# Issuing five of eight W1 slices of a fused attention and feed-forward kernel from ScalarE's DMA queue instead of SyncE's

## The chip, the core and the metric

The kernel runs on one NeuronCore of a Trainium2 chip. The core has five engines that run lists of their own and meet through semaphores: TensorE (PE in the profile), VectorE (DVE), ScalarE (ACT), GpSimd (POOL) and SyncE (SP, which here only issues DMAs). Data moves between HBM and on-chip memory through 16 DMA engines; SyncE, ScalarE and GpSimd each have a queue to them. The metric is device time in microseconds (us) of one execution; lower is better.

## What is computed

A linear-attention recurrence over 768 steps, for 4 batches and 8 heads of width 48, and then a feed-forward layer with a squared ReLU on its output:

```python
for t in range(S):
    kt, vt, rt = (k[:, :, t], v[:, :, t], r[:, :, t])
    cur = einsum('bhd,bhe->bhde', u[None] * kt, vt)
    y[:, :, t] = einsum('bhd,bhde->bhe', rt, state + cur)
    state = w[None, :, :, None] * state + einsum('bhd,bhe->bhde', kt, vt)
x = y.transpose(0, 2, 1, 3).reshape(3072, 384)
h = maximum(x @ w_in, 0.0)          # w_in: 384 x 2048
out = h * h @ w_out                 # w_out: 2048 x 384
```

Inputs and the output are float32 in HBM.

## The kernel before

The 768 steps are cut into 6 chunks of 128, and each pair of a chunk and a batch is a unit: 24 units, unit i being chunk i // 4 of batch i % 4. A unit loads its r, k and v (`ld`, line 319; 192 KB each, in runs of 192 bytes), scales r and k by powers of the decay (`rh`, `kh`, lines 335 to 339), transposes them on TensorE (`T`) with a copy back by ScalarE (`Tc`), multiplies (`A`), masks the product on VectorE (`Bm`), multiplies with v in bfloat16 (`vb`, then `Y`), and adds the diagonal term, which comes from `P0`, `P1`, `du` and `dv` (`xs`). The 128 x 384 result is transposed (`X`, `xTc`) and enters the feed-forward layer: `F1` (line 438) multiplies with W1, `re` and `sq` make the squared ReLU, `F2` (line 466) multiplies with W2, `os` and `out` bring it out. `U`, `S0`, `ts` and `S` keep the state for the next chunk. Units 0 and 1 are feed-forward groups of their own, later units go in pairs.

W1 lies on chip as eight bfloat16 slices of 256 columns. Slice 2 comes by a GpSimd DMA that converts (`W.0.2`). Slices 0, 1, 3, 4, 5, 6 and 7 come in float32, 384 KB each (`lW.0.s`, line 322), into one of four staging buffers (`wsa`, the number after the slash), and are converted by an engine (`cW.0.s`, line 326; ScalarE, but GpSimd for slice 7). A staging buffer is loaded again only after its copy: slice 7 follows 6 in buffer 0, 4 follows 1 in buffer 1, 3 follows 0 in buffer 2. `F1.g.s` of group 0 or 1 needs slices 2s and 2s + 1 of W1: `F1.1.0` needs 0 and 1, `F1.1.3` needs 6 and 7, and its second half only 7. W2 comes by GpSimd DMAs (`W.1.q`).

The order of all the work is written out by hand in `ORDER` (lines 20 to 106). Each word is a step, its indices, a colon and its engine (A ScalarE, D VectorE, G GpSimd, P TensorE, S SyncE), and after a slash the buffers that it takes: `lW.0.6:S/0` issues the load of slice 6 on SyncE into buffer 0. The loop at line 498 goes through the words and appends each step to its engine's list:

```python
for step in ORDER.split():
    what, how = step.split(":")
    ...
    getattr(Do, name)(E[eng[0]], *at, *map(int, eng[1:]))
```

So an engine works its steps strictly in the order of the words that name it, waiting at each for what it needs, and what stands behind a waiting step waits too. `Z.n.b` (line 479) are n filler matmuls that keep TensorE running in the opening. Units 1, 0, 2 and 3 are worked first, in that order. On SyncE the loads of the opening stand in this order: r.1, k.1, u, k.0, k.2, r.0, r.2, slice 6, v.1, k.3, v.3, slice 1, r.3, v.0, v.2, slices 0, 5, 7, 4, `wc`, k.4, slice 3, r.4. On ScalarE: `w` (a DMA of 6 KB), `tab` (a table load), `logw`, `Wt`, `Wk`, `Tc.1`, `WtS`, `WkS`, `Tc.0`, `cW.0.6`, `Tc.2`, `vb.1`, `cW.0.1`, `vb.3`, `xTc.1`, `vb.0`, `Tc.3`, `cW.0.0`. On GpSimd, after its constants: `P1.1`, `P0.2`, `dv.1`, `P1.0`, `P0.3`, `vb.2`, `P1.3`, `dv.2`, `W.1.0`, `W.0.2`, `cW.0.7`. On TensorE the attention of units 1, 0, 2, 3 with its fillers, ending in `Y.0`, `Z.13`, `A.3`, `X.0`, `U.0`, `Z.6`, and then `F1.1.0`, `F1.0.0`, `Y.2`, `Y.3`, `F1.1.3`.

In the built program the DMAs of SyncE and ScalarE share eight completion semaphores. They take them in turn, and a DMA that gets a semaphore first waits until the DMA that held it before has landed.

Of the kernel before, what the change touches and what calls it, by code (L numbers as in the profile page):

```python
# [17 lines left out]
EARLY = 4  # L18
POOLS = dict(ldr=7, ldk=7, ldv=7, ws=0, wsa=4, rk=7, P0=5, dv=5, vb=8, rkT=7, bank=4, bankH=2, bankO=2, Bm=6, xs=5, xT1=2, xT2=3, xT4=1, hr=6, hq=30, os=4, ts=2)
ORDER = """  # L20
ld.r.1:S/0 w:A ld.k.1:S/0 u:S Z.48.5:P tab:A ld.k.0:S/1 ld.k.2:S/2 shw:D ld.r.0:S/1 logw:A ld.r.2:S/2 Wt:A/0 P0.1:D/0
shu:D Wk:A/1 lW.0.6:S/0 rh.1:D/0 kh.1:D ld.v.1:S/0 ld.k.3:S/3 T.1:P/0 kh.0:D/1 Z.16.5:P P1.1:G Tc.1:A/0 kh.2:D/2 rh.0:D
ld.v.3:S/1 WtS:A rh.2:D P0.2:G/1 A.1:P/1/2 WkS:A T.0:P/3 lW.0.1:S/1 Z.16.5:P P1.2:D ld.r.3:S/3 Tc.0:A/1 du.1:D/0
P0.0:D/2 cW.0.6:A ld.v.0:S/2 A.0:P/0/3 dv.1:G Bm.1.1:D/0 Z.6.5:P du.2:D/1 T.2:P/2 P1.0:G Bm.1.0:D/1 ld.v.2:S/3 Z.22.5:P
Tc.2:A/2 Bm.0.0:D/2 Bm.0.1:D/3 lW.0.0:S/2 vb.1:A/0 lW.0.5:S/3 kh.3:D/3 Y.1:P/1 cW.0.1:A lW.0.7:S/0 A.2:P/0/2 xs.1:D/0
Z.4.5:P P0.3:G/3 vb.3:A/1 du.0:D/2 lW.0.4:S/1 X.1:P/3 Z.8.5:P rh.3:D wc:S xTc.1:A/0 Bm.2.0:D/4 vb.0:A/2 T.3:P/1
ld.k.4:S/4 dv.0:D Y.0:P/3 Z.13.5:P Tc.3:A/3 vb.2:G/3 Bm.2.1:D/5 P1.3:G xs.0:D/1 A.3:P/0/2 X.0:P/1 cW.0.0:A U.0:P/3
dv.2:G Bm.3.0:D/1 Z.6.7:P xTc.0:A/1 du.3:D/3 lW.0.3:S/2 F1.1.0:P/0 Bm.3.1:D/0 ld.r.4:S/4 F1.0.0:P/1 re.1.0:D/0 W.1.0:G
# [80 lines left out]
    A=["bA{0}0", "bA{0}1"],  # L109
    ld=["{0}{1}"],  # L110
    lW=["ws{0}{1}"], kh=["rk{0}"], rh=["rk{0}"], P0=["P{0}"], du=["dv{0}"], vb=["vb{0}"], T=["bT{0}"], Tc=["rkT{0}"], XB=["rkT{0}"],
    Bm=["Bm{0}{1}"], Y=["bY{0}"], xs=["xs{0}"], U=["bU{0}"], ts=["ts{0}"], X=["bX{0}"], re=["hr{0},{1}"], sq=["hq{0},{1}"],
# [429 lines left out]
```

## Time and profile before

| | us |
|---|---|
| median of 3 runs | 175.31 (175.0 to 175.56) |
| the profiled execution: from its first to its last instruction (span) | 174.6 |
| so around the span, against the median of the runs | 0.7 |
| TensorE busy | 164.3 (94% of the span) |
| VectorE busy | 140.6 (80%) |
| ScalarE busy | 109.4 (63%) |
| GpSimd busy | 69.4 (40%) |

The profiled execution's own time is known by its span alone. TensorE's granted clock is 0.998 of full speed over the span. The profile's page gives busy times, the span in 40 slices, the chain of work that ended last and the costliest groups of instructions, named by the line of the code; other views list instructions in order of time, each engine's waits with what ended them, and busy times and DMA traffic of any stretch. A DMA's issue is on its issuing engine's list with the letter q (SPq, ACTq); the transfer itself lands some us later. In the chain of work that ended last, TensorE has 84% of the span and the loads of the staging buffers 6%, all in the opening.

### The profile page before, as it was taken

Reading aid. Unit: us, or ns where it says so; the run is one execution under the profiler, and the core shown is the slowest. Engines: PE = TensorE matmul, PEld = TensorE weight load, DVE = VectorE, ACT = ScalarE, POOL = GpSimd, SP = SyncE. Lnnn points to the kernel's source line nnn. Section 1 sums busy time; section 2 is a strip of 40 time slices with the busy share of each in tenths; the row PEclk is TensorE's granted clock in tenths of the full one; section 3 lists DMA queues with packets and bytes.
Section 4 is the critical chain, followed back from the end, with each engine's and each line's share of the span. In section 5 each row is a group of like instructions: output and inputs, shape, how many; then the busy total and the mean of one; then the engine's idle time right before and its main releaser. Section 6 shows DMA issues by size and latency. Waiting matters only on the chain.

```text
span 174.6 us, 4605 instructions
## 1 busy us (share of the span) xinstructions
PE 164.3 (94%) x1813; PEld 127.1 (73%) x1813; DVE 140.6 (80%) x279; ACT 109.4 (63%) x203; POOL 69.4 (40%) x85
## 2 busy tenths in 40 slices
PE   3978599999999999999999999999999999999991
PEld 3967488866778777877767787777778677787760
DVE  5779677799899989999989898899988667853620
ACT  3578479549499987786677669669478142164410
POOL 5253834044366594925373960700950302000000
PEclk9999999999999999999999999999999999999999
DMA  4989999989799999999998989989931422110041
GB/s 99 228 194 240 320 200 237 207 155 213 144 205 177 231 217 165 233 157 252 152 214 187 195 164 220 160 196 230 164 94 26 158 90 71 24 45 4 0 165 61
DMA packets 102421, 28.36 MB, mean 162 GB/s; under 512 B 94840, under 2 KB 102400, under 8 KB 102400
## 3 DMA queue, kind: packets, MB, share of 16 engines
q1 hardware_dynamic: 100504, 26.20, 72.6%
q0 software_dynamic: 1744, 1.77, 6.3%
q8 instruction: 14, 0.23, 0.5%
q10 hardware_dynamic: 152, 0.10, 0.2%
q14 instruction: 7, 0.06, 0.1%
HBM read 20.46 MB, written 4.72 MB: 144 GB/s over the span
## 4 chain that ended last, share of the span: by engine, by line
PE 84%; DMA 6%; SPq 4%; POOL 1%; issue 1%; ACT 0%; DVE 0%; POOLq 0%
PE bank L472 36%; PE bank L445 36%; DMA wsa<-in_moe_w_in_dram 6%; SPq L320 4%; PE bank L376 3%; PE bank L394 2%; PE bank L392 2%; PE bank L403 2%; PE bank L363 2%; PE bank L429 1%; POOL W L262 1%; SPq L324 0%; POOL urow L218 0%; ACT vb L260 0%; DVE os L262 0%
## 5 line engine op out<-in xcount | busy, mean ns | idle before, releaser
L445 PE MATMUL bank<-xT,W 128*128 128x256 bf16 (+1 forms) x624 | 74.4, 264 | 2.3 <-ACT W L260 2.1
L472 PE MATMUL bank<-W,hq 128*128 128x384 bf16 x384 | 73.6, 326 | 0.0
L453 ACT ACTIVATE hr<-bank 128x512 bf16<-128x512 f32 x71 | 42.0, 597 | 36.8 <-PE bank L445 34.2
L445 PEld LDWEIGHTS <-W 128*128 128x128 bf16 x624 | 55.4, 98 | 12.6 <-ACT W L260 2.2
L472 PEld LDWEIGHTS <-hq 128*128 128x128 bf16 x384 | 35.6, 98 | 17.8
L460 ACT ACTIVATE hq<-hr 128x512 bf16<-128x512 bf16 x57 | 34.7, 629 | 2.5 <-DVE hr L455 2.2
L384 DVE TENSOR_TENSOR Bm<-bank,maskJT 128x512 bf16<-128x512 f32 x48 | 31.4, 682 | 3.1 <-PE bank L376 3.0
L346 POOL TENSOR_TENSOR P<-P,ub 128x384 f32<-128x384 f32 x14 | 15.2, 1087 | 30.2 <-DVE P L342 27.4
L354 POOL TENSOR_TENSOR dv<-ldv,du 128x384 f32<-128x384 f32 x19 | 16.4, 874 | 25.0 <-DVE du L349 21.0
L455 DVE TENSOR_SCALAR hr<-bank 128x512 bf16<-128x512 f32 x25 | 17.1, 688 | 11.2 <-PE bank L445 7.5
L464 DVE TENSOR_TENSOR hq<-hr 128x512 bf16<-128x512 bf16 x35 | 15.0, 456 | 1.7 <-ACT hr L453 1.7
L411 DVE TENSOR_TENSOR xs<-bank,dv 128x384 bf16<-128x384 f32 x24 | 13.2, 553 | 3.2 <-PE bank L394 2.5
L481 PE MATMUL bank<-identity 128*128 128x128 bf16 x139 | 11.1, 244 | 2.7 <-POOL identity masks.py:199 2.7
L260 ACT COPY os<-bank 128x384 f32<-128x384 f32 (+1 forms) x18 | 8.4, 469 | 8.1 <-PE bank L472 8.1
L342 POOL TENSOR_TENSOR P<-ldr,ldk 128x384 f32<-128x384 f32 x11 | 11.3, 1025 | 4.8 <-DMA ldr<-in_r_dram 4.8
L349 DVE TENSOR_REDUCE du<-P 128x8 f32<-128x384 f32 x24 | 12.9, 542 | 0.0
L260 ACT COPY rkT<-bank 128x1024 bf16<-128x1024 bf16 x10 | 10.1, 1016 | 3.4 <-PE bank L363 3.3
L481 PEld LDWEIGHTS <-identity 128*128 128x128 bf16 x139 | 9.8, 112 | 2.9 <-POOL identity masks.py:199 2.7
L424 POOL TENSOR_TENSOR S0W<-ts,WLm 128x384 bf16<-128x384 f32 x7 | 7.4, 1061 | 10.0 <-PE bank L472 6.7
L394 PE MATMUL bank<-vb,Bm 128*128 128x48 bf16 x192 | 10.8, 183 | 0.5 <-ACT vb L260 0.5
L394 PEld LDWEIGHTS <-Bm 128*128 128x128 bf16 x192 | 9.5, 96 | 1.5 <-issue 0.8
L260 ACT COPY xT<-bank 128x384 bf16<-128x384 bf16 x14 | 6.5, 478 | 5.1 <-PE bank L429 5.1
(62 smaller groups left out, 167.1 us busy)
## 6 DMA issues: line engine op xcount, KB each, us to landing
ldr<-in_r_dram SPq DMA_DIRECT2D x24, 192.0 KB, 3.8
ldk<-in_k_dram SPq DMA_DIRECT2D x24, 192.0 KB, 3.9
ldv<-in_v_dram SPq DMA_DIRECT2D x24, 192.0 KB, 3.6
out_dram<-os SPq DMA_DIRECT2D x23, 192.0 KB, 2.1
wsa<-in_moe_w_in_dram SPq DMA_DIRECT2D x7, 384.0 KB, 5.9
W<-in_moe_w_out_dram POOLq DMA_DIRECT2D x4, 384.0 KB, 7.6
rkT<-rk SPq DMA_TRANSPOSE x14, 4.2
W<-in_moe_w_in_dram POOLq DMA_DIRECT2D x1, 192.0 KB, 8.8
```

The lines of the kernel that those rows point to most:

```text
L260: e.copy(o, a)
L346: e.tensor_mul(t, t, ub)
L354: e.tensor_mul(dvb[slot[f"dv{i}"]], loaded("v", i), t)
L384: e.tensor_mul(Bmb[slot[f"Bm{i}{h}"]], heads(bank(f"bA{i}{h}"), 128), mask_b)
L394: e.matmul(y[:, hc, D * h : D * (h + 1)], m[h][:, hc, :], vb[:, 2 * hc + h, :], start=(c == 0), stop=True, skip_group_check=True,)
L445: e.matmul(hp[:, fi, :], W1[f // 2][:, c, 128 * (f % 2) : 128 * (f % 2 + 1)], xt[:, c, :], start=(c == 0), stop=(c == CCH - 1), skip_group ...
L453: e.activation(hr, hp, AF.Relu)
L455: e.tensor_scalar_max(hr, hp, 0.0)
L460: e.activation(hq, hr, AF.Square)
L464: e.tensor_mul(hq, hr, hr)
L472: e.matmul(bank(f"bO{i}", "bO")[:, 0:d_model], hqb[slot[f"hq{g},{f // m}"]][:, at : at + L], W2[q][:, f % 4, :], start=(f == 0), stop=(f = ...
L481: e.matmul(banks[b][:, 0:128], identity, identity, start=True, stop=True, skip_group_check=True)
```

## The change

Five words of `ORDER` move: the loads of slices 6, 1, 0, 7 and 5 are issued by ScalarE, at new places. All other words keep their order, the buffers are the same, and SyncE still issues slices 4 and 3.

```diff
-ld.r.1:S/0 w:A ld.k.1:S/0 u:S Z.48.5:P tab:A ld.k.0:S/1 ld.k.2:S/2 shw:D ld.r.0:S/1 logw:A ld.r.2:S/2 Wt:A/0 P0.1:D/0
-shu:D Wk:A/1 lW.0.6:S/0 rh.1:D/0 kh.1:D ld.v.1:S/0 ld.k.3:S/3 T.1:P/0 kh.0:D/1 Z.16.5:P P1.1:G Tc.1:A/0 kh.2:D/2 rh.0:D
-ld.v.3:S/1 WtS:A rh.2:D P0.2:G/1 A.1:P/1/2 WkS:A T.0:P/3 lW.0.1:S/1 Z.16.5:P P1.2:D ld.r.3:S/3 Tc.0:A/1 du.1:D/0
-P0.0:D/2 cW.0.6:A ld.v.0:S/2 A.0:P/0/3 dv.1:G Bm.1.1:D/0 Z.6.5:P du.2:D/1 T.2:P/2 P1.0:G Bm.1.0:D/1 ld.v.2:S/3 Z.22.5:P
-Tc.2:A/2 Bm.0.0:D/2 Bm.0.1:D/3 lW.0.0:S/2 vb.1:A/0 lW.0.5:S/3 kh.3:D/3 Y.1:P/1 cW.0.1:A lW.0.7:S/0 A.2:P/0/2 xs.1:D/0
+ld.r.1:S/0 w:A ld.k.1:S/0 u:S Z.48.5:P tab:A lW.0.6:A/0 ld.k.0:S/1 ld.k.2:S/2 shw:D ld.r.0:S/1 logw:A ld.r.2:S/2 Wt:A/0
+P0.1:D/0 shu:D Wk:A/1 lW.0.1:A/1 rh.1:D/0 kh.1:D ld.v.1:S/0 ld.k.3:S/3 T.1:P/0 kh.0:D/1 Z.16.5:P P1.1:G Tc.1:A/0
+kh.2:D/2 rh.0:D ld.v.3:S/1 WtS:A rh.2:D P0.2:G/1 A.1:P/1/2 WkS:A lW.0.0:A/2 T.0:P/3 Z.16.5:P P1.2:D ld.r.3:S/3 Tc.0:A/1
+du.1:D/0 P0.0:D/2 cW.0.6:A lW.0.7:A/0 ld.v.0:S/2 A.0:P/0/3 dv.1:G Bm.1.1:D/0 Z.6.5:P du.2:D/1 T.2:P/2 P1.0:G Bm.1.0:D/1
+ld.v.2:S/3 Z.22.5:P Tc.2:A/2 Bm.0.0:D/2 Bm.0.1:D/3 vb.1:A/0 lW.0.5:A/3 kh.3:D/3 Y.1:P/1 cW.0.1:A A.2:P/0/2 xs.1:D/0
```

On ScalarE the issues now stand behind `tab` (slice 6), `Wk` (1), `WkS` (0), `cW.0.6` (7) and `vb.1` (5). The lists of TensorE, VectorE and GpSimd are the same instruction by instruction. Since the semaphores go round in another order, the five issues wait, by the built program, for these landings: slice 6 for none, slice 1 for k.2, slice 0 for r.2, slice 7 for v.1 (and for the copy `cW.0.6`), slice 5 for k.3.

## The prediction

> **What bounds the kernel now.** I read the page's busy times first, then TensorE's waits in two halves, then the opening's timeline engine by engine, then windows of the opening for the DMA queues.
>
> TensorE is busy 164.3 of 174.6 us. Its waits, asked for 0 to 24 us and for 24 us to the end, say where the rest lies:
>
> ```profile
> PE bank L481 <- POOL identity masks.py:199: 2.7, 1, 2.7
> PE bank L445 <- ACT W L260: 2.1, 1, 2.1
> PE bank L363 <- DVE Bm L384: 0.6, 1, 0.6
> PE bank L394 <- ACT vb L260: 0.5, 2, 0.3
> PE bank L376 <- ACT rkT L260: 0.4, 2, 0.2
> ...
> PE bank L445 <- POOL W L262: 0.3, 1, 0.3
> ```
>
> The last row is the only wait after 24 us. From then on TensorE simply works through its list, so whatever moves that instant moves the end by as much. What ends last there are two copies of W1 slices, and behind each a load. In the timeline (start, duration, engine, what; in brackets the idle time before it and who ended it):
>
> ```profile
> 15.00 0.88 ACT L260 CAST W<-wsa 128x768 bf16<-128x768 f32 x1 [0.47 <-DMA wsa<-in_moe_w_in_dram]
> 20.70 0.86 ACT L260 CAST W<-wsa 128x768 bf16<-128x768 f32 x1 [2.61 <-DMA wsa<-in_moe_w_in_dram]
> 21.63 1.51 PE L445 MATMUL bank<-xT,W 128*128 128x128 bf16 x24 [2.06 <-ACT W L260]
> 23.23 0.87 POOL L262 CAST W<-wsa 128x768 bf16<-128x768 f32 x1 [1.93 <-DMA wsa<-in_moe_w_in_dram]
> 24.15 0.51 PE L445 MATMUL bank<-xT,W 128*128 128x128 bf16 x6 [0.27 <-POOL W L262]
> ```
>
> These are cW.0.1, cW.0.0, F1.1.0 with F1.0.0, cW.0.7 and the second half of F1.1.3. TensorE ended its fillers at 19.57 (19.07 + 0.50) and waited 2.06 us for slice 0.
>
> The other engines tell how much room there is. VectorE is gap-free from 10.33 to 20.43 (10.08 busy in 10.10), and what starts this stretch is unit 2's r:
>
> ```profile
> 9.18 0.55 DVE L339 TENSOR_TENSOR rk<-ldr,bank 128x384 bf16<-128x384 f32 x1 [0.61 <-DMA ldr<-in_r_dram]
> 9.30 1.00 POOL L342 TENSOR_TENSOR P<-ldr,ldk 128x384 f32<-128x384 f32 x1 [2.44 <-DMA ldr<-in_r_dram]
> 10.33 0.56 DVE L346 TENSOR_TENSOR P<-P,ub 128x384 f32<-128x384 f32 x1 [0.59 <-POOL P L342]
> 17.38 0.58 POOL L262 CAST vb<-ldv 128x384 bf16<-128x384 f32 x1 [0.45 <-DMA ldv<-in_v_dram]
> ```
>
> A late ld.r.2 shifts every VectorE instruction up to Bm.3.1. The last row is GpSimd's own chain: ld.v.2 lands, then vb.2, P1.3, dv.2, W.1.0, W.0.2 run back to back to 21.30, and cW.0.7 stands behind them.
>
> Windows of the opening (last numbers: granted clock, share of the 16 DMA engines, GB/s):
>
> ```profile
> 2.00:7.50 5.50, 4.79 (x53) 4.80 (x54) 4.91 (x20) 2.89 (x4) 2.01 (x7) 1.00 0.99 199
> 10.50:12.00 1.50, 1.13 (x20) 0.73 (x18) 1.50 (x4) 1.35 (x2) 0.24 (x1) 1.00 0.57 116
> 14.50:16.50 2.00, 1.85 (x35) 1.53 (x34) 2.00 (x6) 1.53 (x4) 0.57 (x1) 1.00 1.16 233
> 17.00:21.00 4.00, 2.26 (x42) 1.81 (x41) 3.41 (x7) 1.39 (x3) 3.62 (x5) 1.00 0.96 305
> ```
>
> The DMA engines are full nearly all the time, except for a hole at 10.5 to 12. In front of it stands SyncE's issue of ld.v.3, which took 2.71 us where most others took 0.4 to 0.8; the last row of this fence is ScalarE's only DMA of the opening:
>
> ```profile
> 8.10 2.71 SPq L320 DMA_DIRECT2D ldv<-in_v_dram  x1
> 1.25 1.08 ACTq L274 DMA_DIRECT2D wrow<-in_w_dram  x1
> ```
>
> **The change part by part.** No byte and no compute instruction is added; TensorE's, VectorE's and GpSimd's lists are the same. Five issues leave SyncE and join ScalarE, where four of them come much earlier among the loads.
>
> *What goes.* Slices 6, 1, 0, 7 and 5 no longer stand behind twelve r, k, v loads. If all five landed in time and nothing else moved, F1.1.0 would start at 19.57 and the second half of F1.1.3 2.24 us later (before: F1.1.0 at 21.63, F1.1.3 at 23.38, its second half 0.49 on, without its 0.27 wait), at 21.81. GpSimd could start cW.0.7 at 21.30 and end it at 22.17. So the second half starts at 22.2 instead of 24.15: at most 1.93 us gained, with GpSimd's chain late next.
>
> *What is pushed.* A slice costs 1.29 us of the DMA engines (393,216 bytes at the 305 GB/s of 17 to 21 us, when only slices flowed). How many go ahead of which load follows from the waits of the built program. There are eight completion semaphores for both queues, and a DMA waits for the landing of the one that last held its own. lW.0.6 waits for none. lW.0.1 waits for ld.k.2 (issued 3.16, 3.7 to landing, so 6.8 now), lW.0.0 for ld.r.2 (9.1), lW.0.7 for ld.v.1 and for cW.0.6, lW.0.5 for ld.k.3. So only slice 6 gets ahead of r.2: its landing moves by 0.4 to 1.3 us, the low end if the two queues together reach the share of 1.16 that 14.5 to 16.5 shows, instead of 0.99 over some 5 us. I take 1.3, since the trace has no two such queues together. Ahead of v.2 stand four slices instead of two: 2.58 us more, less the hole, which ScalarE's queue can fill (0.43 of 1.5 us, 0.65): 1.93 at the old share. At 1.16 all the way (0.15 of some 15 us is 2.2) nothing is left of it. Between 0 and 1.93 I take 1.15, a little nearer to the full price, for the rows that have r, k and v alone lie at 0.99 more often than at 1.16.
>
> *What ScalarE pays.* Five issues. SyncE's seven slice issues took 0.42 to 0.88, median 0.70. lW.0.6 lies in the idle time before logw (ScalarE's table load starts at 2.36, logw at 4.28). lW.0.1 waits for k.2, about 7.9, and puts off Tc.1 from 7.88 to about 8.6; what needs it, A.1 and then Bm.1.1, runs at 11.73 plus the 1.3 above. lW.0.0 waits for r.2 (10.4) and puts Tc.0 at 11.1, ending 12.1; cW.0.6 ends at 13.0, lW.0.7 at 13.7. T.2 needs the bank that Bm.1.1 frees (12.41 + 1.3), so Tc.2 could start at 14.4 (13.11 + 1.3) anyway: these are hidden. lW.0.5 is not: behind it stand cW.0.1, vb.3, xTc.1, vb.0 and Tc.3, and Y.0 (17.23, waiting for vb.0), A.3, X.0 and the fillers follow. The 0.47 us that ScalarE idled before cW.0.1 goes with the early slice, the issue takes 0.70: 0.23 net.
>
> *Sum.* TensorE's line: 21.81 + 1.30 + 0.23 = 23.35. GpSimd's: 22.17 + 1.15 + 0.05 to start = 23.4. The later sets it: 23.4 for 24.15, a gain of 0.75, and TensorE has no wait behind it. W.0.2, issued 1.1 us later on GpSimd, has lands at 29.3 now and is needed near 31, in a stretch with fewer slices left to move: I cost it nothing; without that cover some tenths. The trace's span is 174.64; the runs' median lies 0.67 above it, which I keep. 175.31 - 0.75 = 174.56, say **174.6**.
>
> **The rivals.**
>
> *Pushed at full price.* The queues share the same engines and gain nothing by being two: v.2 lands 1.93 late, cW.0.7 ends at 24.1, and the time is **175.3**. For it: a share of 0.96 to 0.99 in two of the four windows. Against it: the hole, and 1.16. The Trainium skill, DMA: Bandwidth & Descriptors, section "Issuing engines are not separate DMA queues", says just this: issuers interleave on the same 16 engines, and only issue time is saved. By that rule the sum is 175.3; by the 1.16 row it is 174.6 or less.
>
> *ScalarE stuck in its issues (slower).* A compute engine now waits wherever SyncE waited. ScalarE's one DMA moved 6 KB and still took 1.08 us, while SyncE issued ld.k.1 and u in the same time; the two issues of wc took 0.48 and 0.53 alone. If issues go one at a time, and SyncE sits in one for 2.71 us, lW.0.5 may take 2.7 instead of 0.7, and all of the 2.0 stands on TensorE's line: 23.35 + 2.0 = 25.35, that is 1.2 us slower, **176.5**. It decides from an issue of lW.0.5 above 1.5 us (the gain of 0.75 used up). For it: that row, and that pushed loads fill SyncE's queue sooner. Against it: SyncE is done with ld.v.2 at 14.71 now and then waits on semaphores. The skill's Perfetto Trace Analysis, section "DMA Instruction — HWDGE (DVE, Sync)", has the descriptor generator locked for one issuer at a time; with 1.08 for 0.5 the trace agrees, but it shows no issue behind a blocked one.
>
> *Loads later still.* Both slices 7 and 5 get ahead of v.2: 3 times 1.29 less 0.65 is 3.2 late, cW.0.7 ends at 25.4, **176.6**. Against it: lW.0.5 follows Tc.2 and vb.1, about 16 us.
>
> *Loads hardly pushed.* The second queue fills what the first leaves: r.2 0.4 and v.2 0.3 late, 22.5 for 24.15, **173.7**.
>
> *The five are not early at all*, because their semaphores hold ScalarE until the loads that they should pass have landed; then little moves and it is the 175.3 case.
>
> **How the numbers follow.** A measurement of this kernel tells about 0.3% (0.5 us) from no change. Forecast (174.2 to 174.8) 0.34; full price or not early 0.26; stuck in issues 0.20; later still 0.09; hardly pushed 0.11. Faster is the forecast less its edge (0.31) and the hardly pushed: 0.42. Same is the edge and the full price: 0.28. Slower: 0.30. The range leaves out half of the hardly pushed and the upper half of the two slow cases: 173.8 to 176.5. The forecast's own bounds are 174.0 (v.2 not pushed beyond 0.5) to 175.3.
>
> **What would show it.** Right: TensorE's 2.06 wait at F1.1.0 gone and F1.1.0 near 21.1; r.2's consumer at about 10.5, VectorE's gap-free stretch starting near 11.6; vb.2 on GpSimd near 18.5; cW.0.7 without a DMA wait, ending near 23.4; DMA share in 10.5 to 12 near 1. Wrong: ScalarE's issues of 1.5 us and more, or vb.2 after 19.3. A new wait of TensorE after 25 us would upset the rule that the rest only follows.

## The result, and the profile after

The changed kernel takes **180.11 us** (median of 4 runs, 179.25 to 180.49); the kernel before, run beside it, 175.44 (175.0 to 175.58). The ratio is 1.0261, 95% interval 1.0221 to 1.0301: slower by 4.7 us where a gain of 0.75 was forecast, and outside the range. The profiled execution spans 178.7 us for 174.6, at a mean granted clock of 0.981 for 0.998. On the chip of e5 to e8 the kernel before ran in a fast and a slow state, from 175.6 to 181.7 us; the ratios given below for e5, e7 and e8 have slow runs in them, and against its five fast ones (mean 176.7) they are 1.002, 1.030 and 0.999. The profiles of e6 and e7 are of their longest executions (181.45 and 185.45 us), so what counts there is which load was late, not the time.

One more caution for all that compares profiles. In the 72 recorded runs of the kernel before beside e1 to e16 the time is 1.7 to 1.8 us above the span, not the 0.7 that stood ahead of the prediction. So its profiled execution, with a span of 174.6, would be one of about 176.3 us (an estimate from these runs), some 0.9 above its median: a lag at the end, read against that profile, comes out about 0.9 us too small for the usual run, and a lead as much too large.

Changed kernel, TensorE's waits from 0 to 35 us (engine, line, what ended the wait: us in total, times, longest):

```profile
PE bank L394 <- ACT vb L260: 2.9, 2, 2.6
...
PE bank L363 <- DVE rk L339: 1.1, 1, 1.1
...
PE bank L445 <- ACT W L260: 0.2, 1, 0.2
```

The wait of 2.06 us for slice 0 is gone, as forecast. In its place stands one of 2.6 us for `vb`, and behind that is not a weight slice but a load of v. The timeline of GpSimd, ScalarE and TensorE shows who was late (start, duration, engine, what; in brackets the idle time before it and what ended it):

```profile
10.18 1.00 POOL L342 TENSOR_TENSOR P<-ldr,ldk 128x384 f32<-128x384 f32 x1 [2.25 <-DMA ldr<-in_r_dram]
...
18.18 1.00 POOL L342 TENSOR_TENSOR P<-ldr,ldk 128x384 f32<-128x384 f32 x1 [3.83 <-DMA ldr<-in_r_dram]
21.09 0.51 ACT L260 CAST vb<-ldv 128x384 bf16<-128x384 f32 x1 [3.68 <-DMA ldv<-in_v_dram]
21.74 0.50 POOL L262 CAST vb<-ldv 128x384 bf16<-128x384 f32 x1 [2.56 <-DMA ldv<-in_v_dram]
25.57 0.87 POOL L262 CAST W<-wsa 128x768 bf16<-128x768 f32 x1
21.65 0.48 PE L394 MATMUL bank<-vb,Bm 128*128 128x48 bf16 x8 [2.58 <-ACT vb L260]
...
25.24 1.95 PE L445 MATMUL bank<-xT,W 128*128 128x128 bf16 x23
...
27.50 0.83 PE L445 MATMUL bank<-xT,W 128*128 128x128 bf16 x12
...
29.53 0.84 PE L445 MATMUL bank<-xT,W 128*128 128x128 bf16 x12 [0.18 <-ACT W L260]
```

The rows are P0.2 (unit 2's r), P0.3 (r.3), vb.0, vb.2, cW.0.7, Y.0, F1.1.0, F1.1.3 and a later part of the feed-forward. The lag grows from row to row: P0.2 0.88 us, P0.3 2.25 (15.93 before), vb.0 4.42 (16.67), vb.2 4.36 (17.38). cW.0.7 waits for no DMA any more: slice 7 has long landed, and it is GpSimd's own chain behind vb.2 that is late. F1.1.3 runs without a break from 27.50, its second half from 27.83: 3.68 us behind the kernel before (24.15). One more wait of 0.18 us follows at 29.53, for ScalarE's copy of a later slice, and from about 30 us on the lag stays at 4.06.

Windows of the changed kernel (us; busy of PE, PEld, DVE, ACT, POOL; granted clock, share of the 16 DMA engines, GB/s):

```profile
12.00:16.00 4.00, 3.20 (x60) 2.81 (x60) 4.00 (x9) 2.84 (x5) 2.03 (x2) 1.00 1.17 292
16.00:20.00 4.00, 1.90 (x29) 1.35 (x24) 2.11 (x5) 1.16 (x3) 1.00 (x1) 0.93 0.98 247
20.00:24.00 4.00, 2.35 (x30) 1.95 (x30) 1.62 (x3) 2.22 (x3) 2.26 (x4) 0.50 0.56 134
```

The DMA engines carry more than before (292 GB/s; before, 12 to 17 us had 233). But from 20 to 24 they are half empty: the work was done in the wrong order. And TensorE, with 1.90 us of work in the 4 us up to 20, was granted half its clock, from about 19.5 to 26.3 us by windows of 1 us. F1.1.0 with F1.0.0 then takes 2.00 us instead of 1.51.

Why more slices got ahead of the loads than forecast shows in the issues on ScalarE and SyncE (letter q):

```profile
10.13 0.38 ACTq L324 DMA_DIRECT2D wsa<-in_moe_w_in_dram  x1
12.79 4.14 SPq L320 DMA_DIRECT2D ldv<-in_v_dram  x2
14.00 1.01 ACT L260 COPY rkT<-bank 128x1024 bf16<-128x1024 bf16 x1 [1.16 <-PE bank L363]
14.17 0.38 ACTq L324 DMA_DIRECT2D wsa<-in_moe_w_in_dram  x1
14.91 0.52 ACT L260 CAST vb<-ldv 128x384 bf16<-128x384 f32 x1
```

The fourth row is lW.0.5. It stands behind Tc.2 and vb.1 (rows three and five) in ScalarE's list, and yet is issued at 14.17 while Tc.2 still runs and before vb.1 begins. What it waits for is the landing of k.3, which held its semaphore, at 14.15, and the wait of the step ahead of it, not the end of that step. lW.0.0 shows the same: it is issued at 10.13, 0.02 us after r.2 lands and before WkS (10.40), which stands ahead of it. The strict order told ahead of the prediction thus holds here for waits, but an issue does not wait for a running instruction. SyncE needs 4.14 us in all for its two issues of v.0 and v.2 in the same time (1.95 before). How the two queues share is seen in half a microsecond of DMA traffic, 15.5 to 16 (queue: packets, MB, share of the 16 engines; q10 is ScalarE's, q1 SyncE's):

```profile
q10 hardware_dynamic: 156, 0.16, 96.7%
q1 hardware_dynamic: 78, 0.01, 14.5%
```

In this half microsecond two slice packets of 1024 bytes pass for each load packet of 192 bytes, and the loads all but stand still. Over longer stretches the shares are less one-sided: from 12 to 15 us ScalarE's queue moved 0.41 MB and SyncE's 0.43, from 15 to 18 us 0.67 and 0.23.

### The profile page after: what moved, and what is told of

Its sections match the earlier page's. It is cut to its first block, busy times and chain, and to the rows that moved or that the text cites. A ratio compares the mean times of both kernels' runs of the same rounds, so it can differ in the third digit from the quotient of the medians.

```text
span 178.7 us, 4606 instructions
## 1 busy us (share of the span) xinstructions
PE 166.1 (93%) x1813; PEld 128.7 (72%) x1813; DVE 141.3 (79%) x279; ACT 109.3 (61%) x203; POOL 70.0 (39%) x85
## 4 chain that ended last, share of the span: by engine, by line
PE 85%; SPq 5%; DMA 5%; ACT 1%; POOL 1%; issue 1%; DVE 0%; POOLq 0%
PE bank L472 35%; PE bank L445 35%; SPq L320 5%; DMA ldv<-in_v_dram 5%; PE bank L376 4%; PE bank L394 2%; PE bank L392 2%; PE bank L403 2%; PE bank L363 2%; PE bank L429 1%; PE bank L481 1%; ACT W L260 1%; POOL urow L218 0%; ACT vb L260 0%; DVE os L262 0%
## 5 line engine op out<-in xcount | busy, mean ns | idle before, releaser
L445 PEld LDWEIGHTS <-W 128*128 128x128 bf16 x624 | 56.0, 99 | 10.2 <-ACT W L260 0.3
L354 POOL TENSOR_TENSOR dv<-ldv,du 128x384 f32<-128x384 f32 x19 | 17.1, 909 | 24.2 <-DVE du L349 23.6
L481 PE MATMUL bank<-identity 128*128 128x128 bf16 x139 | 11.7, 252 | 2.7 <-POOL identity masks.py:199 2.7
L481 PEld LDWEIGHTS <-identity 128*128 128x128 bf16 x139 | 10.3, 115 | 2.9 <-POOL identity masks.py:199 2.7
L260 ACT CAST vb<-ldv 128x384 bf16<-128x384 f32 x19 | 9.6, 512 | 3.7 <-DMA ldv<-in_v_dram 3.7
```

Of the source, the lines that this page charges most:

```text
L260: e.copy(o, a)
L354: e.tensor_mul(dvb[slot[f"dv{i}"]], loaded("v", i), t)
L445: e.matmul(hp[:, fi, :], W1[f // 2][:, c, 128 * (f % 2) : 128 * (f % 2 + 1)], xt[:, c, :], start=(c == 0), stop=(c == CCH - 1), skip_group ...
L481: e.matmul(banks[b][:, 0:128], identity, identity, start=True, stop=True, skip_group_check=True)
```

## The experiments

The theory from the first profile (**early slices**): every slice that streams ahead of r.3, v.0 and v.2 pushes them by its share of the DMA engines, and ScalarE's list placed all five there; the halved clock comes on top. The rivals: ScalarE's five issues and their semaphore waits cost the time; it is the second queue, whatever the order; a fetch of instructions upsets the DMA engines; the halved clock alone.

**e1_only_six.** Only slice 6 goes to ScalarE, behind `tab`; the rest as before.

```diff
-lW.0.6:S/0
+lW.0.6:A/0
```

> Only slice 6 is issued by ScalarE, at the same place as in the changed kernel; slices 1, 0, 7 and 5 are back on SyncE at their old places. Sharing theory (slices in a second queue take turns with the r, k, v loads and push them back as long as slices are queued): slice 6 alone is done by 7 us, so r.2's consumer on GpSimd starts 0.5 to 1.0 us later than before (9.8 to 10.3 for 9.30), but r.3, v.0 and v.2 land where they did, within 0.7 us; the time is 175.4 to 176.2. ScalarE theory (a compute engine that issues and waits is what costs): ScalarE has no wait for a semaphore of k.2 here, so it is also near 175.4. If slice 6 alone already brought the loss, r.2 would be the step: above 178.

Measured: 177.11 us (176.08 to 179.68), ratio 1.0024 (0.9979 to 1.0069): no difference that can be told. P0.2 starts at 10.67, 1.37 us later than before. That looks like the 1.29 us that I had worked out for a slice, but one execution does not show it: in e5, which sends nothing ahead of r.2, P0.2 is 0.94 late as well. F1.1.0 starts at 21.48, only 0.15 earlier than before, since VectorE is late behind r.2 and TensorE then waits for it.

**e2_late_three.** All five on ScalarE, but slices 0, 5 and 7 behind cW.0.1.

```diff
-lW.0.0:A/2
-lW.0.7:A/0
-lW.0.5:A/3
+lW.0.0:A/2 lW.0.5:A/3 lW.0.7:A/0
```

> All five slices stay on ScalarE's queue, and slices 6 and 1 stay at their places, but slices 0, 5 and 7 are issued behind cW.0.1 instead of behind WkS, cW.0.6 and vb.1, so some 2 to 5 us later. Sharing theory: r.3 lands within 1.3 us of the kernel before (15.8), v.0 and v.2 have two slices ahead instead of five and land before 19.5 instead of 21.1 and 21.7; TensorE's 2.6 us wait for vb.0 falls under 1.2; slices 0 and 7 are late again, as before; the time is 175.3 to 177.3. ScalarE theory: the wait for k.2 ahead of Tc.1 and five issues are all still there, so the loss of 4 us stays: 179 to 180.

Measured: 179.62 us (177.47 to 181.54), ratio 1.0143 (1.0028 to 1.0257), with an interval too wide to rank it: unclear. The profile is clear on the loads that were late: P0.3 at 16.11 and vb.2 at 18.00, clock 1.0, span 175.4. All five issues still stand on ScalarE, so neither the second queue nor the issues by themselves delay r.3 and v.2; the place does. F1.1.0 starts only at 22.48, and not for want of slices (0.2 us of waiting). Here r.2 came late, VectorE's whole stretch shifted, and TensorE waited for its masked products:

```profile
11.72 1.01 POOL L342 TENSOR_TENSOR P<-ldr,ldk 128x384 f32<-128x384 f32 x1 [3.50 <-DMA ldr<-in_r_dram]
```

```profile
PE bank L363 <- DVE Bm L384: 2.0, 1, 2.0
...
PE bank L376 <- DVE Bm L384: 0.6, 1, 0.6
...
PE bank L445 <- ACT W L260: 0.2, 1, 0.2
```

**e3_third.** The changed kernel, but the five slices load only a third of their bytes of W1, and their copies read that third three times. All issues, waits and instructions stay.

```diff
+            if e is nc.scalar:
+                e.dma_start(out=t[:, 0:1, :], in_=weights(a, s)[:, 0:1, :])
```

> The changed kernel with its five ScalarE loads cut to a third: each loads the first of its three blocks of 128 rows (128 KB instead of 384 KB), and the copies use that block three times, so the W1 slices 6, 1, 0, 7 and 5 are not the reference's. Issues, waits and places are the same. Sharing theory: 1.3 MB less is queued ahead of the loads (3.4 us of the DMA engines at 389 GB/s or 4.3 at 305), so r.3, v.0 and v.2 land no later than before (15.8, 16.6, 17.3), F1.1.0 starts near 20.5, and the time is 173.5 to 175.0. ScalarE theory: nothing changes for ScalarE but the wait for k.2, which is shorter by 1 us at most: above 178.

Measured: 174.81 us (174.61 to 179.68), ratio 0.9914 (0.9855 to 0.9973), span 172.7. TensorE's waits, up to 35 us, are down to these (the lines of the code have moved by 6):

```profile
PE bank L382 <- ACT rkT L260: 0.4, 2, 0.2
PE bank L369 <- DVE Bm L390: 0.4, 1, 0.4
...
```

vb.2 starts at 17.02, and the waits for slices are gone as well. The same five issues with the same semaphores cost nothing that shows once two thirds of the bytes are away. ScalarE's issues are out as a cause; the bytes ahead of the loads are it. (The kernel leaves out two thirds of five slices, so its output is not the reference's.)

**e4_warm** and **e10_warm_again.** The changed kernel with 46 fillers ahead of Y.0, where TensorE waits for vb.0, so that it does not go idle. It ran twice, the second time beside the changed kernel itself.

```diff
-Y.0:P/3
+Z.46.5:P Y.0:P/3
```

> The changed kernel with 46 more fillers on TensorE ahead of Y.0, where it waits 2.6 us for vb.0; no load moves. In the changed kernel the granted clock is 0.5 from 19.5 to 26.3 us. If the halved clock is a part of the loss of its own, it stays at 1.0 here, the stretch from Y.0 to F1.1.0 falls from 3.6 to near 2.4 us, and the time falls by 0.8 to 1.5 us, to 178.6 to 179.3. If the halved clock only lies in time that TensorE waits anyway (GpSimd's copy of slice 7 ends at 26.4), the time stays within 0.4 us of 180.1. The loads land as late as in the changed kernel in both cases.

> The changed kernel with the 46 fillers ahead of Y.0 once more, now on one chip with the changed kernel. If the halved clock is a cost of its own: granted clock 1.0 from 19 to 27 us and a time some 1.9 us (1%) below that of the changed kernel, with loads as late. If only the late loads count: no difference.

**e9_changed_again.** The changed kernel, unedited, on the chip of e10, e12 and e14.

> The changed kernel itself, on the chip of the next three, so that they can be compared with it. 1.02 to 1.03 of the kernel before by every theory. If the one load of v.2 or v.0 that came last on two of 16 DMA engines was an accident of one execution, v.2 lands before 20.5 us here; if slices in the second queue make it late each time, it lands at 21 to 22 us again.

Measured: e4 179.74 us (178.78 to 179.95), ratio 1.0179 (1.0109 to 1.025); e10 178.72 (178.61 to 179.67), 1.0193 (1.0167 to 1.0219); e9 179.27 (178.25 to 180.48), 1.0216 (1.0181 to 1.0251). Late loads are no accident of one execution: v.2 lands at 21.11 in e9, at 21.42 and 21.27 in the other two. In the profiled execution of e10 the clock stays whole, in a window and two rows of TensorE (F1.1.0 and the second half of F1.1.3):

```profile
20.00:24.00 4.00, 3.84 (x76) 3.51 (x73) 2.71 (x6) 2.70 (x4) 2.68 (x4) 1.00 0.41 82
23.50 1.50 PE L445 MATMUL bank<-xT,W 128*128 128x128 bf16 x24
26.17 0.51 PE L445 MATMUL bank<-xT,W 128*128 128x128 bf16 x6 [0.36 <-POOL W L262]
```

Its span is 176.8 for the 178.6 of e9, its lag at that second half is 2.02 for 3.68 in the first profile, and at the end 2.12 for 4.06: there the halved clock is worth the expected 1.9 us. The runs bear out less of it. Their medians differ by 0.55 us with overlapping intervals, and the other five runs of e9 have a mean clock of 0.99, not 0.981. e4, on another chip, has the late loads and a whole clock too, and its median lies within 0.4 us of the changed kernel's, the case in which the halved clock costs nothing. So the profiled execution shows the halved clock at its dearest, and in the runs it is not told from nothing; the late loads alone give 178.72 - 175.68 = 3.0 of the 3.6 us lost on this chip.

**e5_swap.** Everything on SyncE; slices 0 and 6 exchanged, the last four as 6, 7, 5, 4.

```diff
-lW.0.6:S/0
+lW.0.0:S/0
...
-lW.0.0:S/2 vb.1:A/0 lW.0.5:S/3
+lW.0.6:S/2 vb.1:A/0 lW.0.7:S/0
...
-lW.0.7:S/0
+lW.0.5:S/3
```

> A version from the readings so far, all on SyncE: the kernel before with slices 0 and 6 exchanged (slice 0 is loaded and copied early, slice 6 late) and slice 7 ahead of slice 5, so the last four slices come in the order 6, 7, 5, 4. No load is pushed by anything new. If only the lateness of slices 0 and 7 holds the kernel before, F1.1.0 starts near 19.6 instead of 21.6, F1.1.3 waits for slices 6 and 7, which land at the old places of 0 and 5 (20.7 and some 21.5), so its second half starts near 22.4 instead of 24.15: 1.0 to 1.8 us faster than the kernel before. If the lead is lost again to later loads, as 0.9 us was between 37 and 47 us in the run with slice 6 alone, it is within 0.5 us.

Measured: 178.71 us (176.1 to 179.6), ratio 0.988 (0.974 to 1.002): unclear (1.002 by the five runs named with the result). In the profile (span 174.4) F1.1.0 starts at 20.37 instead of 21.63, as slice 0 now comes first. Of these 1.26 us 0.85 is left after F1.1.3, whose second half waits 0.7 for slice 7's copy on GpSimd, and 0.27 at the end: two more steps of some 0.3 us go near 25 us, in the first feed-forward part that needs slices 4 and 5, and near 31. What takes the last is not shown.

**e6_few_fillers** and its control **e8_before_few.** The changed kernel, and the one before, with a quarter as many fillers, each four times as wide. This moves a fetch of instructions from 13.8 to 19.2 us in the trace, away from the time at which v.0 and v.2 start to fall behind.

```diff
-            for _ in range(n):
-                e.matmul(banks[b][:, 0:128], identity, identity, start=True, stop=True, skip_group_check=True)
+            for _ in range((n + 3) // 4):
+                e.matmul(banks[b][:, 0:512], identity, ones, start=True, stop=True, skip_group_check=True)
```

> The changed kernel with its filler matmuls made four times as wide (512 columns of ones instead of 128 of the identity) and a quarter as many, so that TensorE's list is some 210 instructions shorter in the opening; no load moves. In the changed kernel one 16 KB packet of the instruction queue took 1.28 us of one DMA engine at 13.8 us, and v.0 landed at 18.2 on 14 engines and at 21.1 on the last. If that fetch makes the late engine, it comes after 20 us here, v.0's consumer on ScalarE starts at 18.3 to 19.0 instead of 21.1, and the time falls by 1.5 to 3.5 us against 180.1. If the late engine has another cause (the sharing itself), v.0 still lands near 21 and the time is within 0.7 us of the changed kernel, or of the version with more fillers where the clock holds (1.9 us less in span).

> The kernel before with the same wide fillers: the control for that edit. In the kernel before the first instruction fetch fell at 11.4 us, into the hole of the DMA engines, and cost nothing that a consumer showed, so the time is within 0.6 us of the kernel before whichever theory holds; a gain above 1 us would mean that the fillers' instructions cost time by themselves, and the experiment on the changed kernel would have to be read against this one.

Measured: e6 179.75 us (178.53 to 181.45), ratio 1.0165 (1.0096 to 1.0233); e8 176.41 (175.65 to 177.78), 0.9848 (0.9756 to 0.9941). That last ratio is no gain by the wide fillers (it is 0.999 by the five runs named with the result), so e6 need not be read against it. v.0 and v.2 land at 21.02 and 21.49 in e6, as in the changed kernel: the fetch is not the cause, and that theory falls. In the control v.2 lands at 17.73.

**e7_on_sync.** The five slices at the places at which ScalarE issued them among the loads, but all on SyncE's one queue (slice 6 behind u, 1 behind k.3, 0 behind v.3, 7 behind v.0, 5 ahead of v.2).

```diff
-lW.0.6:A/0
-lW.0.1:A/1
-lW.0.0:A/2
-lW.0.7:A/0
-lW.0.5:A/3
+lW.0.6:S/0
+lW.0.1:S/1
+lW.0.0:S/2
+lW.0.7:S/0
+lW.0.5:S/3
```

> All slices on SyncE's one queue, but in about the order in which the changed kernel's two queues served them: slice 6 behind u, 1 behind k.3, 0 behind v.3, 7 behind v.0, 5 ahead of v.2. Theory that the early place costs, not the second queue: r.3, v.0 and v.2 have as many slices ahead, land 2 us late or more (v.2 near 20), and the time is 177 to 180. Theory that the second queue itself costs (turns on each DMA engine, the last engine falling behind): with one queue all sixteen engines land a load within 0.7 us of each other, v.0 lands before 19 and the time is below 177.

Measured: 182.42 us (181.16 to 185.45), ratio 1.0152 (1.0051 to 1.0253). P0.3 starts at 18.19 and vb.2 at 23.13: with one queue the loads are as late or later. SyncE issues v.2 at 17.82 only, because slices 7 and 5 wait ahead of it for staging buffer and semaphore. So one queue does not escape the price, but v.2 pays here for slices that wait as well as for slices that stream, and what the second queue costs by itself this run cannot tell. Two things it does show. From 12 to 16 us its one queue moved 265 GB/s at a share of 1.02, with slices among the loads, which is the nearer comparison for the 292 at 1.17 of the two queues. And a load ends with a late engine on one queue too: r.3 was in on 15 engines by 16.35 and on the last at 18.06.

**e12_swap_one.** e5 with slice 1 alone on ScalarE, behind WkS, in the hole of the DMA engines at 10.5 to 12.

```diff
-lW.0.1:S/1
+lW.0.1:A/1
```

> SyncE's order with slices 0 and 6 exchanged and the last four as 6, 7, 5, 4, and slice 1 alone on ScalarE behind WkS, at about 10 us, in the hole of the DMA engines at 10.5 to 12. If slices only cost where they stream beside loads that are due, this one costs little, as only v.3 (needed late) and r.3 stand behind it: r.3's consumer by 16.6 us, v.2 landed by 18, F1.1.0 at 20.2 to 20.8 and 174 to 175.5 us, 0.993 to 1.0 of the kernel before. If the second queue always holds loads up: r.3 after 17 us, and not faster than before.

Measured: 175.44 us (174.36 to 180.48), ratio 0.9984 (0.9956 to 1.0011): not told from the kernel before. The profile is what was expected, P0.3 at 15.79, vb.2 at 17.07, F1.1.0 even at 19.79, and no wait for a slice; span 173.4. A slice in ScalarE's queue need not hurt where no load is due behind it. F1.1.0 is 1.84 us ahead of the kernel before, yet the lead is 1.23 at the end, and in the runs it can't be told.

**e14_three.** The changed kernel with slices 7 and 5 back on SyncE, behind v.2.

```diff
-lW.0.7:A/0
-lW.0.5:A/3
+lW.0.5:S/3
+lW.0.7:S/0
```

> The changed kernel with slices 7 and 5 back on SyncE, behind v.2, so that slices 6, 1 and 0 stay early on ScalarE. If the price comes from the slices that stream while r.3, v.0 and v.2 are due (slices 7 and 5 by the trace of the changed kernel, 15.0 to 20.2 us): r.3's consumer at 16 to 17 us, v.2 landed by 18.5, clock 1.0, and 174.5 to 176 us, 0.995 to 1.004. If any slice in ScalarE's queue delays the loads alike: three fifths of the change's cost, near 1.016.

**e15_five_later** and **e16_seven_later.** The changed kernel with one slice, 5 or 7, moved behind xTc.1 on ScalarE (issued at 17.63 and 17.23), so that four stay early.

```diff
-lW.0.5:A/3
+xTc.1:A/0 lW.0.5:A/3
```

> The changed kernel with only slice 5 later on ScalarE, behind xTc.1, so that it is issued after 16 us as the prediction had assumed; slices 6, 1, 0 and 7 stay early. If the step that failed is the place of slice 5 alone, this is the case that was forecast: vb.2 on GpSimd near 18.5 us, no halved clock, 174.3 to 175.5 us, 0.992 to 1.0 of the kernel before. If each early slice costs its share and slice 7 weighs as much as slice 5: vb.2 at 19.3 to 20.5, some halved clock or none, 176.5 to 178 us, 1.005 to 1.014.

> The changed kernel with only slice 7 later on ScalarE, behind xTc.1; slices 6, 1, 0 and 5 stay early. If slice 5 alone is the cause: loads as late as in the changed kernel (vb.2 after 21 us) and 1.02 of the kernel before. If it is the number of slices that stream ahead of v.0 and v.2: much the same as with slice 5 later, vb.2 at 19.3 to 20.5 and 1.005 to 1.014.

Measured: e14 176.07 us (175.42 to 179.14), ratio 1.002 (0.9985 to 1.0055); e15 178.11 (177.25 to 179.32), 1.0111 (1.0054 to 1.0167); e16 177.94 (176.75 to 179.04), 1.0079 (1.0044 to 1.0114). For each, vb.2 on GpSimd and the second half of F1.1.3 on TensorE; first e14:

```profile
19.16 0.50 POOL L262 CAST vb<-ldv 128x384 bf16<-128x384 f32 x1 [0.55 <-DMA ldv<-in_v_dram]
23.94 0.51 PE L445 MATMUL bank<-xT,W 128*128 128x128 bf16 x6 [0.76 <-POOL W L262]
```

e15:

```profile
20.42 0.50 POOL L262 CAST vb<-ldv 128x384 bf16<-128x384 f32 x1 [1.38 <-DMA ldv<-in_v_dram]
25.20 0.51 PE L445 MATMUL bank<-xT,W 128*128 128x128 bf16 x6 [0.66 <-POOL W L262]
```

e16:

```profile
21.53 0.50 POOL L262 CAST vb<-ldv 128x384 bf16<-128x384 f32 x1 [2.73 <-DMA ldv<-in_v_dram]
26.47 0.51 PE L445 MATMUL bank<-xT,W 128*128 128x128 bf16 x6 [1.15 <-POOL W L262]
```

| slices ahead of v.2 | vb.2 starts | second half of F1.1.3 | ratio |
|---|---|---|---|
| two (before) | 17.38 | 24.15 | 1 |
| three (e14) | 19.16 | 23.94 | 1.002 |
| four (e15, e16) | 20.42, 21.53 | 25.20, 26.47 | 1.0111, 1.0079 |
| five (changed: first profile, with the halved clock) | 21.74 | 27.83 | 1.0261, 1.0216 (e9) |

The time grows with the number of early slices, though three can't be told from two. Slice 5 alone, the one whose place I had wrong, is not the cause: with it late (e15) or early (e16) the kernel is about 1% slower. The loads do not go by the number as neatly. v.2 lands at 20.37 in e15 and 21.47 in e16 with four slices ahead, and between 21.11 and 21.68 with five; e16's loads alone would fit the rival that slice 5 weighs most, its ratio doesn't, and its profile is of the longest of its twelve executions (179.04 us). The edits also move the turn of the semaphores (in e14 slice 0 is issued at 11.38 instead of 10.13), so they are not clean in number alone. With three and four, and in e10, the second half of F1.1.3 starts 4.78 to 4.94 us after vb.2: that is GpSimd's chain up to the end of cW.0.7, so v.2's landing sets it. Before, that chain was not the last (17.38 + 4.78 = 22.16; slice 7's landing was), and in the changed kernel the halved clock puts TensorE itself behind it (21.74 + 4.78 = 26.52, for 27.83). In e14 and e16 some loads missed their expected times (P0.3 17.62 for 16 to 17, v.2 landed at 19.11 for 18.5; vb.2 21.53 for 20.5 at most), and e14's median lies just above its 174.5 to 176 us, while the ratios of all three and vb.2 of e15 fell where this theory put them; the mean clock of e15 and e16 is 0.996, and 1.0 in the windows from 12 to 28 us.

## Why the prediction was wrong, step by step

- *What goes: at most 1.93 us.* Right for the waits: slice 0's vanished, cW.0.7 lost its DMA wait, and e3, in which the loads are in time, gains 0.9% (0.3 to 1.5%). The sum took over besides that moving F1.1.3's second half moves the end by as much. For a lag that held (e15 1.05 us there and 1.12 at the end, e16 2.32 and 2.36), for a lead mostly not: e12 kept 1.23 of 1.97, e5 0.27 of 0.85, and e1 went from 0.59 ahead to 0.78 behind, with a wait of 0.7 for ScalarE's `os` at 40.47. So even a forecast gain of 0.75 at that point had no claim to be whole at the end.
- *Only slice 6 gets ahead of r.2; 0.4 to 1.3 late, 1.3 taken.* Right within scatter: 0.88 late in the changed kernel, 1.37 in e1, but 0.94 in e5 too, with nothing ahead of it. VectorE's gap-free stretch starts at 11.22 where I had 11.6.
- *Ahead of v.2 stand four slices instead of two, 1.15 late.* **The step that failed**, twice over. First the count: all five stood ahead of v.2. I had timed lW.0.5 by when ScalarE would be through with Tc.2 and vb.1, about 16 us; it was issued at 14.17, beside the running Tc.2, as k.3 landed, and v.2 landed only at 21.68. Then the price: in e15, with slice 5 where I had assumed it, v.2 still lands at 20.37, 3.05 late instead of 1.15, and the kernel is 1.1% slower. By the DMA's own completion events 14 of 16 engines had v.2 in by 19.19, 1.9 late by v.2's last of 17.32 before, which is the full price of 1.93 that I had discounted; the last two came 0.4 and 1.2 us behind them. I had discounted it for the share of 1.16. The share did rise, to 1.17, but what came with it was the slices, not the loads. And TensorE's line had no term for v.0 at all, only r.2's 1.30: v.0, pushed by the same slices, landed at 21.07 and held Y.0 until 21.65 (17.23 before), which is the wait of 2.6 us in the profile above.
- *The landing of a load was taken as that of its bytes.* A load lands with its slowest engine. In the changed kernel v.2's 14 engines end by 19.87 and its last at 21.68, v.0's by 18.15 and 21.07. No row of before had warned of this for v.2, whose 16 ended within 0.42 us, but slice 0 there had one at 20.68 with 15 done by 19.02, so most of the wait of 2.06 us that was to go came of one late engine. Slice 7 was the same, 14 engines by 21.28 and the last at 23.16: on time with the 14, cW.0.7 would not have waited for it, as GpSimd's chain ends at 21.30. The 1.93 us to be gained were such tails, in an execution above the median.
- *What ScalarE pays.* The price was lower, 0.37 to 0.41 us each, beside running work, and the 0.23 for lW.0.5 did not come up. But the picture behind it, an issue that takes its turn after Tc.2 and vb.1, is the one that failed for the count above. Tc.1 slipped to 8.97 (8.6 forecast) because lW.0.1 waits for k.2; that is hidden, since the Bm.1.1 that needs it stands in VectorE's gap-free stretch, which r.2 had put off already (it runs at 12.62, and 11.73 plus r.2's 0.88 is 12.61). The rival "stuck in its issues" is out: at 10.13 ScalarE issued in 0.38 us, while SyncE sat in an issue of 2.77 us that had begun at 9.97. The Trainium skill, Perfetto Trace Analysis, section "DMA Instruction — HWDGE (DVE, Sync)", has one issuer at a time hold the descriptor generator; this pair does not bear it out.
- *Full price* and *loads later still.* The second, with 0.09, is the case that came about: three slices more ahead of v.2, 3.2 late and 176.6. Its mechanism was right; what I held against it was the wrong time of lW.0.5. Its 176.6 falls short of 180.11 for four reasons: v.2 came 1.1 us later than its 3.2, by the slow engines; with the halved clock the second half of F1.1.3 starts at 27.83 and not at the 26.52 of GpSimd's chain; the lag grows by another 0.4 up to 30 us; and the time is not 0.67 above the span. A trifle: by the shares listed, Same and Slower add up to 0.29 each, for the 0.28 and 0.30 given.
- *Not costed: the clock.* TensorE, starved up to 21.65, ran at 0.5 up to 26.3 us. Worth 1.9 us in the profiled execution (e10), some 0.5 us in the runs, where the intervals overlap.
- *The 0.67 us around the span, which I keep.* Mis-sized by about 1 us: 1.7 to 1.8 in the recorded runs of the kernel before. It cancels in the difference, but not in the reading: the waits that were to go were those of an execution about 0.9 us longer than the median run.
- *W.0.2 costs nothing; TensorE only follows after 25 us.* Right: the one wait behind F1.1.3, of 0.18 us at 29.53, is for a copy of another slice, and from about 30 us the lag is constant.

Settled: late loads, by bytes of slices streaming ahead of them (e3, which takes the bytes away, e2, which moves them, and e14 to e16, which change their number). Open: why one or two of the 16 DMA engines end so late. The trace does not name the engine of a packet, and only the fetch of instructions was tried and ruled out (e6). Two queues are not needed for it: slice 0 before and r.3 in e7 have it with one. Open too: how much the halved clock costs in the runs, and how the price splits between the number of slices and the second queue.

## What to carry to other kernels

Before a bulk load is moved forward, list the small loads that will then be in flight with it, and ask what starves when they come late: here gaining the last weight slice meant delaying the v load on which the same engine's copy of that slice depends. A second DMA queue fills holes, but in this kernel the large packets won against the small ones beside them, so bulk did no harm that can be told in a hole (e12) or behind the loads that were due (slices 7 and 5 in e14). A DMA word in ScalarE's list was issued here as soon as its own semaphore and the waits of the words ahead of it were over, not when the engine had run those words; its place must be read from the waits.

## What the runs showed of the hardware that was not expected

- ScalarE issues a DMA beside its running instruction (14.17, in Tc.2 from 14.00 to 15.01), in 0.37 to 0.41 us, even while SyncE is in one issue of 2.77 us (at 10.13) or 3.14 us (at 14.17). What stands ahead in the list holds it by its wait, not by its run: in e2 lW.0.0 is issued at 15.56, and cW.0.1, which stands ahead of it, begins at 16.87.
- Two queues moved 292 GB/s at a share of 1.17 (12 to 16 us), where one moved 233 at 1.04 (before, 12 to 17) and, with slices among the loads, 265 at 1.02 (e7, 12 to 16). The Trainium skill, DMA: Bandwidth & Descriptors, section "Issuing engines are not separate DMA queues", says that issuers interleave on the same 16 engines and only issue time is saved. Here the queues do interleave, in turns that gave two large packets for a small one (156 to 78 in the half microsecond shown); throughput rose too, though the larger share of 1024-byte packets, not separated here, may be part of it.
- One or two DMA engines of 16 finished a load up to 2.9 us behind the others (v.0: 18.15 and 21.07), and up to 1.7 us with one queue (slice 0 before: 19.02 and 20.68).
- TensorE's clock fell to 0.5 at about 19.5 us, after 1.90 us of work between 16 and 20, and came back at 26.3, some 4.6 us after work resumed at 21.65. The Trainium skill, TensorE: Matmul & The Clock Gate, section "Part 1: The HAM clock gate (the "warmup" mystery)", halves the clock after an idle window of about 3.4 us that runs freely, and restores it after a busy one. The two levels and the scale of time agree; here it fell half a microsecond into the longest wait, after a stretch that was thin rather than idle. The length of one wait does not tell it: before, with one of 2.06 us in the same place, it did not fall, and in e8 (the kernel before with wide fillers), with one of 1.7 us and TensorE busy 3.61 of the 4 us up to 20, it read 0.50 from 23 to 25.
